# A decode attention block with its gradients: steps of two heads instead of four, with another order of work

## The chip, the cores and the metric

The kernel runs on one core of a Trainium2 chip. The core has five engines that run side by side, each through its own list of instructions in order: TensorE (PE, with a separate row PEld for its weight loads), VectorE (DVE), ScalarE (ACT), GpSimd (POOL) and SyncE (SP). SP and POOL here also issue the transfers, which 16 DMA engines carry out. The metric is the device time in microseconds (us), as a median of several executions. The profile shows one execution, and times in it count from its first instruction.

## The reference

One decode step (one token for each of two batches) of an attention block and a bilinear MLP beside it, and then the gradients with respect to all inputs. Both read the same normalized `x`.

```python
xn = layernorm(x)                                   # 2 x 576
q = (xn @ wq) as 32 heads of 128                    # two query heads per KV head
scores = q . k_cache / sqrt(128)                    # k_cache: 2 x 16 x 4096 x 128
p = softmax(scores);  o = p @ v_cache
out = x + o @ wo + ((xn @ w_gate) * (xn @ w_up)) @ w_down      # F = 4608
# and, from grad_out: gradients of x, k_cache, v_cache, wq, wo, w_gate, w_up, w_down
```

The caches are bf16, 32 MB each, and their gradients are as large. Each cache gradient is an outer product: for one KV head, 4096 x 128 numbers come from the two query rows with 4096 probabilities (for V) or score gradients (for K). So the kernel reads 92.48 MB and writes 92.48 MB. The arithmetic on a byte is small, but every number of the gradients has to pass through PSUM.

## The kernel before

**Steps.** `G = 4` KV heads of one batch make a step; there are `NGRP * Bq = 8` steps. Their order is a Python loop at the end of the kernel. A step does this:

1. `head_scores` (K): load a head as one 1 MB transfer (L469, issued by SP) into a tile of 128 partitions x 4096; transpose it in 32x32 blocks on VectorE (L102, tile `X`); add its scores into PSUM tile `ps_sc` with 16 matmuls (L475) whose weights `W` are 128x128 and whose moving side has 256 columns. All four heads go into one 128x256 tile.
2. `softmax`: maxima, exponential on ScalarE, sums; the probabilities `pr`, and their transpose `pT`, made by VectorE.
3. The same `head_scores` for V, which gives the gradient of the probabilities; `contract` (L488) multiplies V by `pT`, 32 matmuls a head, each writing one of four strips of 32 PSUM partitions. The strips are added up by an fp32 matmul with a constant, `contract_end` (L497, `R40`, four per call).
4. `dscores` makes the score gradients `ds` and `dsT`; then `contract` of K with `dsT`.
5. `outer_units`: the cache gradients. For one pair of blocks, four matmuls (L512) multiply 32 rows of `pr` or `ds` by 32 rows of `BD`, a masked copy of the queries or of the output gradient, with 512 columns. They fill two PSUM tiles `ps_o` of 128x1024, one for each `aa`, that is for each group of 32 rows; ScalarE (L93) or VectorE (L90) casts them into the store tiles `so`; `evac` chooses by a running sum of costs. When a tile is full, POOL issues the store of 1 MB (L519). It holds a quarter of the tokens of four heads, so that a piece of 2 KB is contiguous in memory.

```python
for h in range(2):
    for aa in range(2):
        a = 2 * A + aa
        nc.tensor.matmul(o[aa][:, h, :], lhsT=rows[32 * a:32 * a + 32, P * h:P * (h + 1)],
                         rhs=BD[t][32 * a:32 * a + 32, cq, :], start=True, stop=True)
```

**Around the steps.** `mlp_units` works through the MLP in nine slices of 512 columns, with loads (L272 to L275), transposes (`Xw`, `Xd`), matmuls and gradient stores `stw`, `std`, `stt`; `group_front` and `back_units` do the same for the slices of `wq` and `wo` (1152 KB and less, stores `stq`, `sto`). These units and the outer products lie in two lists, `side` and `outs`; `fill` takes some from each between the heads of a step.

**What sets the order.** The tile framework orders the instructions of each engine and inserts the waits. Buffers come from pools by tag: 11 tiles `nat` hold heads and weights alike, 2 tiles `X`, 4 tiles `st` for stores, and in PSUM 2 `m`, 2 `sc` and 2 `o`. `build_BD` makes `BD` by a matmul (L456), a ScalarE cast (L458) and four VectorE masks of 128x512 (L461). SP executes its loads in order: a load whose tile is not free holds those behind it.

Of the kernel before, what the change touches and what calls it, by code (L numbers as in the profile page):

```python
# [13 lines left out]
P = 128  # L14


def view(t, p0, np_, off, dims):

    (pstep, _), *_ = t.ap
    return bass.AP(t.tensor, t.offset + p0 * pstep + off, [[pstep, np_], *[list(d) for d in dims]])  # L20


@with_exitstack
def kernel(
# [30 lines left out]
    G = 4  # L55
    GH = 2 * G
    NGRP = Hkv // G
    NIT = NGRP * Bq
    NCH = Sk // P
    WW = 24 + P  # L60
# [7 lines left out]
    HD2 = D // 2  # L68

    const = ctx.enter_context(tc.tile_pool(name="const", bufs=1))  # L70
    sb = ctx.enter_context(tc.tile_pool(name="sb", bufs=1))
    ps = ctx.enter_context(tc.tile_pool(name="ps", bufs=1, space=bass.MemoryType.PSUM))

    def ps_m(shape, dtype=FP32):
        return ps.tile(list(shape), dtype, tag="m", bufs=2, name="ps_m")

    def ps_sc():
        return ps.tile([P, 256], FP32, tag="sc", bufs=2, name="ps_sc")

    def ps_o():  # L80
        return ps.tile([P, 2, 512], FP32, tag="o", bufs=2, name="ps_o")

    load = {"v": 0.0, "s": 0.0}

    def evac(out, in_, cols):
        cv = 0.16 + cols * 0.00104
        cs = 0.19 + cols * 0.00083
        if load["v"] + cv < load["s"] + cs:
            load["v"] += cv
            nc.vector.tensor_copy(out=out, in_=in_)  # L90
        else:
            load["s"] += cs
            nc.scalar.copy(out, in_)  # L93

    def dve(us):
        load["v"] += us

    def act(us):
        load["s"] += us
# [4 lines left out]
    def pairs(ap):  # L104
        return ap.bitcast(FP32)


    ident = const.tile([P, P], BF16, name="ident")
    make_identity(nc, ident[:])
    identf = const.tile([P, P], FP32, name="identf")  # L110
    nc.vector.tensor_copy(identf[:], ident[:])

    def sums(name, dims, off=0):

        n = dims[0][1]
        t = const.tile([P, n], FP32, name=name)
        nc.vector.reduce_sum(t[:], view(identf[:], 0, P, off, dims), axis=AX.X)
        return t

    R8 = sums("R8", [[1, 8], [8, 16]])  # L120
    G8 = const.tile([P, 16, 8], FP32, name="G8")
    nc.vector.tensor_copy(G8[:], view(R8[:], 0, P, 0, [[0, 16], [1, 8]]))
    R40 = sums("R40", [[1, 8], [40, 4]])
    F8 = sums("F8", [[1, 8], [32, 4]])
    Q4 = sums("Q4", [[32, 4], [1, 32]])
    C16 = sums("C16", [[8, 16], [1, 8]])
    maskc = const.tile([P, 4], FP32, name="maskc")
    nc.vector.reduce_sum(maskc[:], view(C16[:], 0, P, 0, [[1, 4], [4, 4]]), axis=AX.X)
    mask8 = const.tile([P, 4, 2], FP32, name="mask8")
    nc.vector.tensor_copy(mask8[:], view(Q4[:], 0, P, 0, [[1, 4], [0, 2]]))  # L130

    sel = const.tile([P, 4, 4, 32], BF16, name="sel")
    selA = const.tile([P, 4, 4, 32], BF16, name="selA")
    for be in range(4):
# [3 lines left out]
    nc.vector.memset(one1[:], 1.0)  # L138

    x_bf = sb.tile([2, D], BF16, tag="st", bufs=4, name="x_bf")  # L140
    nc.sync.dma_start(x_bf[:], A_x.rearrange("b s d -> (b s) d"))
    dy_bf = sb.tile([2, D], BF16, tag="st", bufs=4, name="dy_bf")
    nc.sync.dma_start(dy_bf[:], grad_out.rearrange("b s d -> (b s) d"))
    x_f = sb.tile([2, D], FP32, tag="X", bufs=2, name="x_f")
    nc.vector.tensor_copy(x_f[:], x_bf[:])

    mu = const.tile([2, 1], FP32, name="mu")
    nc.vector.reduce_sum(mu[:], x_f[:], axis=AX.X)
    nc.vector.tensor_scalar(mu[:], mu[:], 1.0 / D, None, op0=ALU.mult)
    xn_f = sb.tile([2, D], FP32, tag="nat", bufs=11, name="xn_f")  # L150
    nc.vector.tensor_scalar(xn_f[:], x_f[:], mu[:], None, op0=ALU.subtract)
    xsq = sb.tile([2, D], FP32, tag="X", bufs=2, name="xsq")
    var = const.tile([2, 1], FP32, name="var")
    nc.vector.tensor_tensor_reduce(
        out=xsq[:], in0=xn_f[:], in1=xn_f[:], scale=1.0 / D, scalar=0.0,
        op0=ALU.mult, op1=ALU.add, accum_out=var[:],
    )
    eps_t = const.tile([2, 1], FP32, name="eps_t")
    nc.vector.memset(eps_t[:], EPS)
    rstd = const.tile([2, 1], FP32, name="rstd")  # L160
    nc.scalar.activation(rstd[:], var[:], AF.Sqrt, bias=eps_t[:], scale=1.0)
    nc.vector.reciprocal(rstd[:], rstd[:])
    nc.vector.tensor_scalar(xn_f[:], xn_f[:], rstd[:], None, op0=ALU.mult)
    xn_bf = sb.tile([2, D], BF16, tag="st", bufs=4, name="xn_bf")
    nc.vector.tensor_copy(xn_bf[:], xn_f[:])

# [5 lines left out]
    for src, dst in ((dy_bf, dyr), (xn_bf, xnr)):  # L172
        o = ps_o()
        for k in range(2):
            nc.tensor.matmul(o[:, k, 0:HD2], lhsT=sel2[:].rearrange("b a m -> b (a m)"),
                             rhs=src[0:2, k * HD2:(k + 1) * HD2], start=True, stop=True)
        nc.vector.tensor_copy(dst[:].rearrange("p (k n) -> p k n", k=2), o[:, :, 0:HD2])


    xs = const.tile([P, 6, 32], BF16, name="xs")  # L180
    nc.gpsimd.memset(xs[:], 0.0)
    tp = ps_m([P, 6, 2], BF16)
    for c in range(4):
        nc.tensor.transpose(tp[:, c, :], xn_bf[0:2, c * P:(c + 1) * P], ident[0:2, 0:2])
    nc.tensor.transpose(tp[0:64, 4, :], xn_bf[0:2, 512:576], ident[0:2, 0:2])
    nc.tensor.transpose(tp[:, 5, :], xn_bf[0:2, 448:576], ident[0:2, 0:2])
    nc.vector.tensor_copy(xs[:, 0:4, 0:2], tp[:, 0:4, :])
    nc.vector.tensor_copy(xs[0:64, 4, 0:2], tp[0:64, 4, :])
    nc.vector.tensor_copy(xs[64:128, 5, 0:2], tp[64:128, 5, :])


    Wdy = const.tile([P, NB, 2, P], BF16, name="Wdy")
    nc.gpsimd.memset(Wdy[:], 0.0)
    dyT = sb.tile([P, 2 * NB, 32], BF16, tag="X", bufs=2, name="dyT")
    t32(dyT[:].rearrange("p k m -> p (k m)"), view(dyr[:], 0, P, 0, [[64, NB], [1, 2], [2, 32]]))
    for a in range(4):
        nc.vector.tensor_copy(
            view(Wdy[:], 32 * a, 32, 32 * a, [[P, 2 * NB], [1, 2]]), dyT[32 * a:32 * a + 32, :, 0:2])

    W = [const.tile([P, 4, G, WW], BF16, name=f"W{t}") for t in range(2)]  # L200
    dM = const.tile([P, 2, G, P], BF16, name="dM")
    for t in range(2):
        nc.gpsimd.memset(W[t][:], 0.0)
    nc.gpsimd.memset(dM[:], 0.0)
    BD = [const.tile([P, 4, G * Dh], BF16, name=f"BD{t}") for t in range(2)]
    Wms = [const.tile([P, 35, 8], BF16, name=f"Wm{i}") for i in range(2)]
    Wts = [const.tile([P, 19, 8], BF16, name=f"Wt{i}") for i in range(2)]
    oTs = [const.tile([P, 2, GH, 32], BF16, name=f"oT{i}") for i in range(2)]
    for t in (*Wms, *Wts, *oTs):
        nc.gpsimd.memset(t[:], 0.0)  # L210
    nwm = [0]


    acc = const.tile([P, 5, 2], FP32, name="acc")
    nc.vector.memset(acc[:], 0.0)
    accx = const.tile([P, 160], FP32, name="accx")
    nc.vector.memset(accx[:], 0.0)

    def nat(shape, name):
        return sb.tile(list(shape), BF16, tag="nat", bufs=11, name=name)  # L220

    def xtile(shape, name):
        return sb.tile(list(shape), BF16, tag="X", bufs=2, name=name)

    def stile(shape, name):
        return sb.tile(list(shape), BF16, tag="st", bufs=4, name=name)

    def tailtile(name):
        return sb.tile([P, FS], BF16, tag="stt", bufs=2, name=name)


    def stationaries(rep, half):

        i = nwm[0] % 2
        nwm[0] += 1
        Wm, Wt = Wms[i], Wts[i]
        nc.vector.tensor_tensor(
            view(Wm[:], 0, P, 0, [[8, 32], [2, 4], [1, 2]]), view(rep, 0, P, 0, [[2, 32], [0, 4], [1, 2]]),
            view(mask8[:], 0, P, 0, [[0, 32], [2, 4], [1, 2]]), ALU.mult)
        for h in range(2):  # L240
            off, dims = half(h)
            n = len(dims) > 1 and dims[0][1] or 1
            nc.gpsimd.tensor_copy(
                view(Wt[:], 64 * h, 64, 0, [[P // n, n], [1, P // n]]), view(Wm[:], 64 * h, 64, off, dims))
        dve(0.4)
        return Wm, Wt

    def dxn(Wm, Wt, X, pos, xoff, xstep):

        dp = ps_m([P, 160])  # L250
        for s in range(8):
            for q in range(4):
                nc.tensor.matmul(dp[32 * q:32 * q + 32, 0:P], lhsT=view(Wm[:], 0, P, 8 * pos(q, s), [[1, 32]]),  # L253
                                 rhs=view(X[:], 0, P, xoff(q, s), [[xstep, 4], [2, 32]]),
                                 start=(s == 0), stop=(s == 7))
# [6 lines left out]
        dve(0.35)  # L262


    def mlp_units(i):
        f0 = i * FS
        m = {}

# [67 lines left out]
        def outer_gu(w):  # L336
            def f():
                hb = m["hb"]
                if w == 0:
                    m["st"] = stile([P, 8, FS], "stw")  # L340
# [330 lines left out]
    def fill(no, ns):  # L671
        for _ in range(min(no, len(outs))):
            outs.pop(0)()
# [139 lines left out]
```

## Time and profile before

| what | value |
|---|---|
| median of 3 runs | 670.47 us (668.05 to 681.68) |
| span of the profiled execution | 666.9 us |
| mean granted TensorE clock in it | 0.716 |
| bytes read and written | 92.48 MB and 92.48 MB |
| mean transfer rate | 279 GB/s |
| scores (L475) | 1024 matmuls of 256 columns, 189.7 us busy |
| outer products of the caches (L512) | 512 matmuls of 512 columns, 173.3 us busy |
| ScalarE casts of 128x1024 for `so` | 222, 1019 ns each |
| VectorE transposes of K and V | 64, 2299 ns each |

A row of groups names the line, the engine, the operation, the tiles (output <- inputs) and the count; then the busy time, the mean of one instruction in ns, and the idle time ahead of them with what ended it. The rows in tenths cut the span into 40 equal slices; `PEclk` is the share of full speed that TensorE's clock was granted. The page's chain of waits is followed back from the last instruction. A matmul's end is modelled, and matmuls overlap, so its busy time is not its cost in a sequence; the distance from one start to the next is.

### The profile page before, as it was taken

The page shows a single profiled execution, that of the slowest core. Times are in us where ns is not written, and L with a number is a line of the kernel's source. Part 1 is how long each engine was busy: PE and PEld are TensorE (multiplying, and loading weights), DVE is VectorE, ACT ScalarE, POOL GpSimd, SP SyncE. Part 2 cuts the span into 40 slices and gives each one's busy share as a digit, 9 for nine tenths or more (in the row PEclk, how much of TensorE's full clock was granted, in tenths as well). Part 3 has the DMA queues.
Part 4 walks back from the last instruction along what each step waited for, and adds up shares of the span by engine and source line. Part 5 has one row for each costly group of instructions (what it writes and reads, how often), then busy time and mean ns, then how long its engine had stood idle before and what let it go on. Part 6 is the DMA issues. An engine that isn't in the chain of part 4 may idle for free.

```text
span 666.9 us, 14489 instructions
## 1 busy us (share of the span) xinstructions
PE 574.7 (86%) x6297; PEld 298.5 (45%) x6297; DVE 360.4 (54%) x499; ACT 330.7 (50%) x445; POOL 129.8 (19%) x252
## 2 busy tenths in 40 slices
PE   1679997897989999897999999899796999989954
PEld 1455553545534445444543454355553345453411
DVE  8686245546594246636484345637287134862245
ACT  0145655283555545374445635456362655645441
POOL 6131201131121121221122221112022111201111
PEclk9998868597886558598776557578597556885555
DMA  8965989559959879749949969829977688834355
GB/s 296 373 234 189 364 325 371 185 178 420 393 201 340 325 246 339 291 154 408 388 163 365 321 249 348 312 83 362 403 280 267 228 295 326 305 133 166 128 197 197
DMA packets 52824, 185.89 MB, mean 279 GB/s; under 512 B 4077, under 2 KB 19065, under 8 KB 44569
## 3 DMA queue, kind: packets, MB, share of 16 engines
q1 hardware_dynamic: 28392, 92.49, 38.4%
q0 software_dynamic: 24368, 92.48, 37.4%
q8 instruction: 49, 0.80, 0.5%
q14 instruction: 15, 0.11, 0.1%
HBM read 92.48 MB, written 92.48 MB: 277 GB/s over the span
## 4 chain that ended last, share of the span: by engine, by line
PE 49%; issue 15%; DMA 10%; ACT 9%; DVE 8%; POOL 1%; ACTq 0%; POOLq 0%; DVEq 0%
PE ps_o L512 16%; PE ps_sc L475 14%; DMA out_dram<-so 10%; ACT so L93 7%; PE ps_m L488 5%; DVE X L102 3%; PE ps_m L497 2%; PE ps_o L379 2%; PE ps_o L345 2%; DVE so L90 1%; PE ps_m L253 1%; PE ps_m L417 1%; DVE Xw L102 1%; PE ps_o L655 1%; DVE stq L90 1%
## 5 line engine op out<-in xcount | busy, mean ns | idle before, releaser
L93 ACT CAST so<-ps_o 128x1024 bf16<-128x1024 f32 x222 | 217.1, 1019 | 174.2 <-PE ps_o L512 116.7
L475 PE MATMUL ps_sc<-X,W 128*128 128x256 bf16 x1024 | 189.7, 328 | 13.2 <-DVE negb L540 7.7
L102 DVE STREAM_TRANSPOSE X<-kv 128x2048 f32<-128x2048 f32 x64 | 147.0, 2299 | 47.0 <-PE ps_sc L475 21.1
L475 PEld LDWEIGHTS <-W 128*128 128x128 bf16 x1024 | 103.9, 113 | 82.8 <-issue 55.2
L512 PE MATMUL ps_o<-BD,pr 32*128 32x512 bf16 x256 | 91.6, 488 | 6.2 <-ACT so L93 4.4
L512 PE MATMUL ps_o<-BD,ds 32*128 32x512 bf16 x256 | 81.7, 487 | 12.0 <-ACT so L93 3.5
L519 POOL DMA_DIRECT2D out_dram<-so x64 | 48.9, 765 | 193.9 <-ACT so L93 91.8
L90 DVE CAST so<-ps_o 128x1024 bf16<-128x1024 f32 x34 | 41.4, 1218 | 49.1 <-PE ps_o L512 43.3
L488 PE MATMUL ps_m<-kv,dsT 128*32 128x128 bf16 x1024 | 29.4, 285 | 11.4 <-ACT o_sb L491 11.4
L93 ACT CAST stw<-ps_o 128x1024 bf16<-128x1024 f32 x33 | 32.6, 1017 | 11.6 <-PE ps_o L345 9.7
L488 PE MATMUL ps_m<-kv,pT 128*32 128x128 bf16 x1024 | 38.2, 257 | 0.1
L488 PEld LDWEIGHTS <-pT 128*32 128x32 bf16 x1024 | 20.3, 107 | 36.1 <-issue 33.5
L488 PEld LDWEIGHTS <-dsT 128*32 128x32 bf16 x1024 | 23.1, 128 | 29.3 <-issue 27.7
L512 PEld LDWEIGHTS <-ds 32*128 32x128 bf16 x256 | 14.7, 96 | 37.3 <-issue 32.0
L497 PEld LDWEIGHTS ps_m<-R,o_sb 128*128 128x128 f32 x128 | 25.7, 281 | 11.0 <-issue 5.7
L93 ACT CAST std<-ps_o 128x576 bf16<-128x576 f32 x33 | 20.7, 640 | 18.8 <-PE ps_o L379 14.4
L497 PE MATMUL ps_m<-R,o_sb 128*128 128x2 f32 x128 | 27.7, 321 | 2.6 <-DVE cr L566 2.6
L512 PEld LDWEIGHTS <-pr 32*128 32x128 bf16 x256 | 15.7, 97 | 25.3 <-issue 16.9
L491 ACT COPY o_sb<-ps_m 128x128 f32<-128x128 f32 x64 | 17.0, 278 | 20.1 <-PE ps_m L488 19.8
L458 ACT CAST bd<-ps_m 128x512 bf16<-128x512 f32 x16 | 9.4, 587 | 30.7 <-PE ps_m L456 30.6
L379 PE MATMUL ps_o<-dyr,hb 32*128 32x288 bf16 x72 | 19.3, 365 | 4.8 <-ACT std L93 4.7
L261 DVE TENSOR_TENSOR accx<-accx,ps_m 128x160 f32<-128x160 f32 x13 | 4.0, 309 | 35.9 <-PE ps_m L258 35.9
(180 smaller groups left out, 578.4 us busy)
## 6 DMA issues: line engine op xcount, KB each, us to landing
out_dram<-so POOLq DMA_DIRECT2D x64, 1024.0 KB, 7.5
kv<-in_A_k_cache_dram SPq DMA_DIRECT2D x32, 1024.0 KB, 8.4
kv<-in_A_v_cache_dram SPq DMA_DIRECT2D x32, 1024.0 KB, 8.8
out_dram<-stw POOLq DMA_DIRECT2D x18, 512.0 KB, 8.1
wd<-in_B_w_down_dram SPq DMA_DIRECT2D x9, 576.0 KB, 8.2
out_dram<-std POOLq DMA_DIRECT2D x9, 576.0 KB, 4.4
wo<-in_A_wo_dram SPq DMA_DIRECT2D x4, 1152.0 KB, 9.4
wgu<-in_B_w_gate_dram SPq DMA_DIRECT2D x9, 512.0 KB, 9.9
```

Of the source, the lines that this page charges most:

```text
L90: nc.vector.tensor_copy(out=out, in_=in_)
L93: nc.scalar.copy(out, in_)
L102: nc.vector.transpose(out, in_)
L345: nc.tensor.matmul(o[a // 2][:, a % 2, dc * P:(dc + 1) * P], lhsT=xnr[32 * a:32 * a + 32, dc * P:(dc + 1) * P], rhs=hb[32 * a:32 * a + 32, ...
L379: nc.tensor.matmul(o[aa][:, k, 0:HD2], lhsT=hb[32 * a:32 * a + 32, 0, :], rhs=dyr[32 * a:32 * a + 32, k * HD2:(k + 1) * HD2], start=True, ...
L458: nc.scalar.copy(bd[:], bp[:].rearrange("p l d -> p (l d)"))
L475: nc.tensor.matmul(s_ps[:], lhsT=view(W[t][:], 0, P, (be * G + l) * WW + 24 - 8 * cq, [[1, P]]), rhs=view(X[:], 0, P, 2 * cq * Dh + 64 * ( ...
L488: nc.tensor.matmul(o_ps[32 * cq:32 * cq + 32, :], lhsT=rowsT[:, 4 * h + c4, :], rhs=head[:, 8 * c4 + 2 * cq + h, :], start=(h == 0 and c4 ...
L491: nc.scalar.copy(o_sb[:, l, :], o_ps[:])
L497: nc.tensor.matmul(t_ps[:, 2 * l:2 * l + 2], lhsT=o_sb[:, l, :], rhs=R40[:, 2 * l:2 * l + 2], start=True, stop=True)
L512: nc.tensor.matmul(o[aa][:, h, :], lhsT=rows[32 * a:32 * a + 32, P * h:P * (h + 1)], rhs=BD[t][32 * a:32 * a + 32, cq, :], start=True, sto ...
L519: nc.gpsimd.dma_start(oview[b, 2 * A + aa, :, G * g:G * g + G], m["st"][aa][:].rearrange("p l c d -> p l (c d)"))
```

## The change

Most of the kernel is written anew. What it does:

- `G = 2`: a step has two heads of K and two of V, and there are 16 steps.
- **Scores in four column tiles.** `score` issues 32 matmuls a head with weights of 32 columns and a moving side of 128; four in a row (`cq`) write the four strips of 32 partitions of one 128x128 PSUM tile.
- **`spread`** replaces the VectorE transposes of `pr` and `ds`: 32 small matmuls with a permuted identity make both the transposed and the spread rows; one cast takes them from PSUM (`pp`, `dd`).
- **Contraction** of both V heads and both K heads in one go at the end of the step, each in one column tile, with two columns of weights; one fp32 matmul a step follows. The four head tiles are released after it.
- **Head stores.** A store tile holds one head as it lies in memory: one partition has 32 tokens, 8 KB. The unit of the outer product has two matmuls for two groups of 32 rows, into the two halves of one PSUM tile. The store is issued by SP.
- **`BD`** is made in one GpSimd product of 128x2048 for a step and side.
- **Fixed rings** in place of pools: 9 head tiles `kv`, 5 weight tiles `ww`, 1 `gu`, 3 `X`, 4 `st`, 3 `BD`, in PSUM 2 `o`, 2 `m`, 1 `sk`, 1 `sv`.
- **Order.** Every part is a Python generator that yields what it needs (an engine with a cost, a free slot, an event). The class `Order` advances them by a list schedule with these costs, while the kernel is built; under `manual_schedule` the instructions of an engine keep that order on the chip.

```diff
+class Order:
+    HOP = 0.12
+    BW = 410e3
+    SLACK = 0.15
...
+    def run(self):
+        while self.streams:
...
+            t0 = min(c[0] for c in cand)
+            t, s, e = min((c for c in cand if c[0] <= t0 + self.SLACK), key=lambda c: (c[1].prio, c[0]))
...
+def EV(cols, bias=0.25):
+    return ("any", [("ACT", 0.19 + cols * 0.00083, 0.0), ("DVE", 0.16 + cols * 0.00104, bias)])
...
+NKV, NX, NGU, NWW, NST, NBD = 9, 3, 1, 5, 4, 3
+MLP0, MLPD = 5, 6.5
+KVSTORE = "SP"
...
-    G = 4
+    G = 2
...
+    def put(engine, parts, tag, slot, events=()):
+        def run():
+            for j, (dst, src, nbytes) in enumerate(parts):
+                yield DMA(engine, 0.77 if engine == "POOL" else 0.6, nbytes)
+                (nc.gpsimd if engine == "POOL" else nc.sync).dma_start(dst, src)
+            yield ("lrel", tag, slot)
...
+    def unit(mms, pe, cols, ev, store):
+        i = yield ACQ("o")
+        yield PE(pe)
+        mms(o_t[i])
+        e = yield EV(cols)
+        ev(e, o_t[i])
+        yield REL("o", i)
+        yield from store.done()
...
+    def load_kv():
...
+                    i = yield ACQ("kv")
+                    yield DMA("SP", 0.6, 1 << 20)
+                    nc.sync.dma_start(kv_t[i][:], views[t][b, G * g + l])
...
+                    for h in range(2):
+                        yield DVE(1.25)
+                        t32(pairs(X_t[x][:, 2048 * h:2048 * h + 2048]), pairs(src[:, 2048 * h:2048 * h + 2048]))
...
+                yield POOL(4.5)
+                nc.gpsimd.tensor_tensor(BD_t[i][:], view(vr_t[v][:], 0, P, 0, [[0, 16], [1, Dh]]),
+                                        view(mask16[:], 0, P, 0, [[1, 16], [0, Dh]]), ALU.mult)
...
+    def score(t, s, sc, l):
...
+        for be in range(4):
+            for c2 in range(2):
+                for cq in range(4):
+                    nc.tensor.matmul(
+                        sc[32 * cq:32 * cq + 32, :],
+                        lhsT=view(W[:], 0, P, (be * G + l) * WW + 6 - 4 * c2 - 2 * l, [[1, 32]]),
+                        rhs=view(X[:], 0, P, (2 * cq + c2) * Dh + 64 * (be // 2) + be % 2, [[8 * Dh, 4], [2, 32]]),
...
+    def spread(src, dst_ps):
+        for c4 in range(4):
+            for a in range(4):
+                blk = src[:, 32 * c4:32 * c4 + 32]
+                rows = identP[:, 32 * a:32 * a + 32]
+                nc.tensor.matmul(dst_ps[32 * a:32 * a + 32, 32 * c4:32 * c4 + 32], lhsT=blk, rhs=rows,
+                                 start=True, stop=True)
...
+    def head_outer(s, t, l, pr2, done):
+        i = yield ACQ("st")
...
+        store = Store(4, put(KVSTORE, [(oviews[t][b, G * g + l], st[:], 1 << 20)], "st", i, ()))
+        def mk(A, h2):
+            def mms(o):
+                for k in range(2):
+                    c4 = 2 * A + k
+                    nc.tensor.matmul(o[:, k, :], lhsT=pr2[32 * c4:32 * c4 + 32, :],
+                                     rhs=BD[32 * c4:32 * c4 + 32, 8 * l + 4 * h2:8 * l + 4 * h2 + 4, :],
+                                     start=True, stop=True)
...
+    def contract(s):
...
+        heads = [(S["ppT"], kvS[s][1][l], l) for l in range(G)] + [(S["ddT"], kvS[s][0][l], l) for l in range(G)]
+        for part in range(4):
+            yield PE(0.95)
...
+            for c in range(8 * part, 8 * part + 8):
+                for j, (rT, slot, l) in enumerate(heads):
+                    nc.tensor.matmul(ct[32 * j:32 * j + 2, 0:P], lhsT=rT[:, 4 * c + 2 * l:4 * c + 2 * l + 2],
+                                     rhs=kv_t[slot][:, Dh * c:Dh * (c + 1)], start=False,
+                                     stop=(c == NCH - 1), skip_group_check=True)
+        for t in range(2):
+            for l in range(G):
+                yield REL("kv", kvS[s][t][l])
...
+    with tc.manual_schedule():
+        od.spawn(front(), (-1.0,))
+        od.spawn(load_ws(), (-0.5,), 1.2)
+        od.spawn(load_kv(), (0.0,), 1.2)
+        od.spawn(turn(), (1.0,))
...
+        od.spawn(attend(), (0.0,))
+        od.spawn(dscores(), (0.0,))
+        od.spawn(backs(), (1.2,))
+        od.run()
```

The arithmetic stays the same, as do the bytes read and written.

## Prediction

> **What bounds the kernel now.** I read the busy row, then the clock and DMA rows, then the queues and the chain that ended last.
>
> ```profile
> PE 574.7 (86%) x6297; PEld 298.5 (45%) x6297; DVE 360.4 (54%) x499; ACT 330.7 (50%) x445; POOL 129.8 (19%) x252
> ...
> PEclk9998868597886558598776557578597556885555
> DMA  8965989559959879749949969829977688834355
> ...
> q1 hardware_dynamic: 28392, 92.49, 38.4%
> q0 software_dynamic: 24368, 92.48, 37.4%
> ...
> PE 49%; issue 15%; DMA 10%; ACT 9%; DVE 8%; POOL 1%; ACTq 0%; POOLq 0%; DVEq 0%
> ```
>
> TensorE is busy for 86%, often at a granted clock of half speed. The transfers need 38.4% + 37.4% + 0.6% = 76.4% of the span, 509 us of 666.9. So the DMA engines are the floor, and 158 us of their time is lost. Windows of 10 us (columns: us, PE, PEld, DVE, ACT, POOL busy, clock, DMA share, GB/s) show where:
>
> ```profile
> 130.00:140.00 10.00, 9.79 (x100) 5.49 (x99) 2.99 (x4) 5.44 (x6) 1.42 (x6) 0.76 0.01 2
> ...
> 150.00:160.00 10.00, 8.32 (x136) 5.43 (x135) 8.50 (x13) 4.50 (x6) 2.15 (x5) 0.83 1.02 424
> ...
> 220.00:230.00 10.00, 10.00 (x110) 4.84 (x106) 2.87 (x7) 6.67 (x9) 2.23 (x3) 0.50 1.00 352
> 230.00:240.00 10.00, 10.00 (x71) 3.69 (x71) 4.58 (x6) 4.16 (x6) 1.90 (x6) 0.50 0.52 200
> ```
>
> While TensorE is full, DMA goes from saturated to nothing. The reader is to see that the two hinder each other. SyncE's own waits name the link:
>
> ```profile
> SPq L469 <- PE ps_m L488: 171.4, 29, 20.2
> SPq L469 <- DVE Xw L102: 72.9, 4, 24.2
> ```
>
> A head's load waits 171 us in all for the contraction that frees its buffer. A step holds 8 heads, and the 11 `nat` buffers are shared with the weights.
>
> **TensorE, part by part.** The spacing of matmuls comes from pieces of the chain (start, length, what), all in stretches at clock 0.5:
>
> ```profile
> 133.20 0.97 PE ps_o L512 x4
> ...
> 226.47 0.96 PE ps_o L512 x2
> ...
> 392.64 2.57 PE ps_m L488 x92
> ...
> 402.76 3.31 PE ps_sc L475 x15
> ```
>
> *Scores.* 1024 matmuls of 256 columns, 3.31/15 = 0.22 us each: 225 us if all ran at half clock. They become 2048 of 128 columns in four column tiles. L488 has that shape, 2.57/92 = 0.028 us, so 57 us; minus 168. The trace mixes clocks (189.7 us busy), so in it they shrink to about 48.
>
> *Outer products.* Still 512 matmuls of 512 columns. Two of them cost 0.96 us now when both use the same 32 rows (`h` runs inside one PSUM tile), but four cost 0.97 when row groups alternate. The new unit always pairs two row groups into one PSUM tile: 256 pairs at 0.485, 124 us at half clock; against 173.3 in the mixed trace, about 95.
>
> *Smaller.* The fp32 reduction L497 falls from 128 matmuls (27.7 us) to 16: 5 us. The 1024 new matmuls of 32 columns in `spread` have a near row, L258 (32 columns, column tiles): 16 in 0.26 us; 16 us, at most 29 if they cost like L488. Sixteen short softmax chains instead of eight add 32 fp32 matmuls, 0.3 us each: 10. The rest keeps its work, 574.7 - 189.7 - 173.3 - 27.7 = 184 us. Sum 48 + 95 + 5 + 16 + 10 + 184 = **358 us**; at half clock throughout (184 becomes about 220), 57 + 124 + 8 + 25 + 10 + 220 = **444**. Both lie under the DMA floor, so TensorE stops being the bound, whichever clock is granted.
>
> **The other engines.** ScalarE: the order of its instructions in the changed kernel has 284 evacuations of 1024 columns (264 now) at 1.019, 289 us, 61 of 576 at 0.64, 39, and some 40 us of small copies and exponentials: about 370 against 330.7. VectorE loses the 64 masks (19.1) and the transposes of probabilities (7); halving the K and V transposes costs 64 fixed shares, (2 x 1373 x 1024/1152 - 2299) ns = 0.14 us each, 9 us; double chains add 18, and 13 fewer large casts take 16 away: about 345. GpSimd gets 32 products of 128x2048 that no row shows. Below, its memset of 128x2432 takes 2.27 us, so 1.9. The Trainium skill, "GPSIMD Engine Reference", section on elementwise cost, prices a two-input product of 2048 fp32 elements at 4.5 us; I take that, and twice it as the upper end: 144 us, 61 to 288. With 49 us of head stores gone from its queue, POOL stands near 230. Three BD buffers put these products beside the previous step.
>
> **A rule against this.** The skill's "SBUF — State Buffer", section "two separate sides", says that a GpSimd operation locks a port pair, and VectorE operations with two SBUF inputs or in a two-port mode wait for all of it. The row first: the K transpose runs at 2299/2048 = 1.12 ns per element, the pace of casts out of PSUM (1218/1024 = 1.19), so it shows no use of a second port. The exposed operations are 33 small ones (`pr`, `hb`, `qr`). By the rule GpSimd holds the lock for 144/560 of the time, mean rest 2.25 us: 33 x 0.26 x 2.25 = 19 us of VectorE; by the rows, nothing. VectorE has 200 us spare; both leave the total.
>
> **DMA.** The bytes are unchanged, 185 MB. Loads in mostly 8 KB rows cost 38.4% for 92.49 MB, stores in 2 KB pieces 37.4% for 92.48: long rows buy nothing measurable; I take zero, with 3% of the stores' share (8 us) for the ends. The skill's "DMA: Bandwidth & Descriptors", specifications, limits a core to about 358 GB/s from HBM; that would make 185/0.358 = 517 us. The windows with DMA share about 1 run at 352 to 426, most near 375 to 400; 375 gives 493. I take the row.
>
> What matters is whether loads can run on. A step now holds 4 heads, and 9 buffers are theirs alone: while one step waits for its contraction, five heads of the next ones can land. Waiting for L488 should mostly go. Next late is the queue itself.
>
> **Moved work.** The 64 head stores leave POOL for SP. SP executes in order: a store waiting for ScalarE holds every load and weight behind it, and a load waiting for PE holds the stores. The order gives four loads, then about four stores, so each delay is one burst. In the same ring a store also lands after the loads ahead of it. The four `st` buffers are filled 107 times (64 heads, 43 weight gradients): over 535 us each filling may last 20. It fills in 4 x 1.02 us, is issued in 0.8, and lands in 7.5 now (page, head stores), say 13 behind part of a burst: 18. It fits, barely.
>
> **The sum.** After the last exponential ScalarE's order still holds 57 casts of 1024 columns and 13 of 576, 58 + 8 + 3 for small ones = 69 us. The last store and the final row arithmetic follow: from the last `stqt` cast at 655.8 to the end it is 11 us now; with a 1 MB landing, 16. Tail 85 us, against 73 now (no score matmul after 594). In those 69 us some 20 MB move. Before them 166 MB must move: 166/0.375 = 443 us, plus 4 us of a slow start. For in-order waits I add 5% of it, 25 us. 4 + 443 + 25 + 85 = **557 us of span**. The executed median is 670.5 for a span of 666.9, so 3.6 lie around it: **560 us**, 110 us less. If the stalls vanish it is 535; if head stores are truly cheaper, 527; with 15% stalls, 602.
>
> **Rivals.**
> *One ring, four store buffers* (slower). If a store regularly lands behind a whole burst of 4 heads and 1.6 MB of weights, that is 5.6/0.375 = 15 us more: hold 4.1 + 0.8 + 22.5 = 27.4, and 107 x 27.4/4 = 733 us. It decides over the DMA from a hold of about 21, and passes today's time at 25. For it: ScalarE waits already 13.2 us for `out_dram<-so`, and that link is 10% of the chain. Against it: the stores overlap three other fillings, and bursts are half as long as steps today.
> *Part of the idle stays* (less gain). Loads still come in fours after a contraction that frees K and V together; if bulk transfer runs at 320 GB/s, between today's mean of 279 and full: 166/0.32 + 89 + 4 = 612.
> *It doesn't do what it says.* The waits only move to SP behind stores and DMA stays at today's 280 to 290: 166/0.285 + 93 = 675, near no change. Against it: the buffer count per step more than doubles.
>
> **Chances.** Forecast (527 to 602) 0.62; 612 case 0.20; no change 0.07; one-ring case 0.11. Range 520 to 640, which leaves out the last two. Two per cent, 657 to 684, is what a measurement of this kernel can tell from no change: faster 0.82, same 0.07, slower 0.11.
>
> **What would show it.** Right: score matmuls near 30 ns apart, PE busy below 450 us, DMA share above 85% before the tail, few SP waits on the contraction, ScalarE closing the kernel for about 70 us. Wrong: ScalarE or VectorE waiting for `out_dram<-st` by more than 60 us (one ring), GpSimd products above 9 us, DMA windows below 0.1 in mid-kernel, or head stores landing in more than 20 us.

## The result, and the profile after

Time after: **639.16 us** median of 4 runs (633.71 to 640.21), against 669.26 us for the kernel before in the same session. The ratio is 0.957, with a 95% interval of 0.949 to 0.965. Some executions of the kernel before are in a slower state, and the ratios here and below compare the others. The kernel is faster by 4%, where 16% were forecast: 30 us of 110. The profiled execution has a span of 638.4 us, at a mean granted TensorE clock of 0.584 (0.716 before).

The rows of the page after, the same ones that the prediction shows of before:

```profile
PE 452.2 (71%) x8489; PEld 270.5 (42%) x8489; DVE 355.1 (56%) x643; ACT 344.5 (54%) x470; POOL 204.8 (32%) x289
...
PEclk9976565765557565755555565655557555556555
DMA  8949989693998749986963969896938965493661
...
q1 hardware_dynamic: 40424, 159.61, 65.4%
q0 software_dynamic: 7024, 25.37, 10.4%
```

TensorE lost 122 us of busy time, although its clock fell. The transfers need about the same share as before: 65.4% + 10.4%, and 0.8% for two small queues, are 76.6%, 489 us instead of 509. No row of an engine is full, and yet only 29 us of span are gone. The waits of SyncE's queue after:

```profile
SPq L477 <- ACT st L309: 226.1, 37, 19.3
...
SPq L810 <- PE ps_o L953: 31.9, 4, 18.0
...
SPq L810 <- PE ps_o L508: 21.0, 3, 9.2
SPq L810 <- PE ps_m L939: 16.2, 2, 8.3
SPq L810 <- PE ps_m L1092: 10.7, 2, 6.1
SPq L810 <- PE ps_m L1000: 9.2, 2, 8.9
```

Only one of these rows names the contraction (L1092), but the names mislead. The profile infers who ended a wait from what TensorE was doing just then. A head tile `kv` is read by TensorE in the contraction alone, and the times agree. Here is one case, the last matmuls of a contraction and the next head load (start us, us, what):

```profile
233.53 0.22 PE L1092 MATMUL ps_m<-kv,dd 128*2 128x128 bf16 x2
...
233.80 0.34 SPq L810 DMA_DIRECT2D kv<-in_A_k_cache_dram  x1
```

All 13 waits of over 1 us ahead of a head load, 97 us together, end within 0.05 us of the end of a contraction, that of two steps before. In the kernel before, 209 us of such waits end so. They are halved, then, and not gone, and the heads still come in bursts of about four. Ahead of them in the queue stand the stores (L477), which wait for their casts. Whether that costs anything, the first experiment tells.

**Where the time is.** I cut each span at the end of the last exponential, as the prediction did: 588 us before, 535 us after. The windows (us, busy time of PE, PEld, DVE, ACT, POOL, clock, DMA share, GB/s) of before:

```profile
0.00:588.00 588.00, 517.96 (x5751) 275.12 (x5751) 327.03 (x447) 297.94 (x403) 118.04 (x234) 0.74 0.81 296
588.00:667.00 79.00, 56.76 (x549) 23.43 (x547) 33.35 (x53) 32.74 (x42) 11.81 (x18) 0.55 0.42 153
```

and of after:

```profile
0.00:535.00 535.00, 382.04 (x7583) 239.00 (x7583) 318.81 (x576) 280.20 (x393) 179.51 (x266) 0.60 0.81 307
535.00:638.00 103.00, 70.17 (x908) 31.48 (x906) 36.30 (x68) 64.25 (x79) 25.29 (x23) 0.52 0.55 215
```

The first part became 53 us shorter, and the tail gave 24 us of it back. In the tail ScalarE has 64 us of work instead of 33: the outer products that the list ranks last have piled up there (100 of the 512 matmuls of L953, where 64 of L512 were left before). In the first part TensorE went from 88% busy to 71%, so its freed time became idle time, not speed. The transfers still run at a mean share of 0.81.

One piece of TensorE's timeline after (start us, us, what, idle time before it and its releaser) shows what it does in such idle time:

```profile
384.70 0.61 PE L953 MATMUL ps_o<-BD,pp 32*128 32x512 bf16 x2 [0.42 <-ACT st L309]
385.61 0.61 PE L953 MATMUL ps_o<-BD,pp 32*128 32x512 bf16 x2 [0.30 <-ACT st L309]
386.52 0.61 PE L953 MATMUL ps_o<-BD,pp 32*128 32x512 bf16 x2 [0.31 <-ACT st L309]
387.44 0.61 PE L953 MATMUL ps_o<-BD,pp 32*128 32x512 bf16 x2 [0.31 <-ACT st L309]
```

A unit of two matmuls comes every 0.91 us, not every 0.485. There are two PSUM tiles `o`, and each is free again only when its cast has ended. TensorE works in order, so all that is listed behind the unit stands with it. The window row of this stretch, and VectorE's next instruction, tell what sets the pace:

```profile
384.50:388.30 3.80, 2.44 (x8) 0.44 (x9) 0.00 (x0) 3.80 (x5) 1.08 (x2) 0.50 0.94 335
...
392.00 1.23 DVE L311 CAST st<-ps_o 128x1024 bf16<-128x1024 f32 x1 [9.08 <-DMA out_dram<-st]
```

ScalarE casts for all of the 3.80 us, one cast every 0.90 us, and VectorE does nothing: its next cast waits 9.08 us for a store to land and free its store tile. So in this burst the casts on one engine are the limit, and more PSUM tiles alone would not have made it quicker. From 376 to 438 us no score is computed at all; bursts like this one, MLP and projection work, and waits for their weights fill that stretch.

### The profile page after: what moved, and what is told of

Read it like the earlier page. It is cut to its first block, busy times and chain, and to the rows that moved or that the text cites. A ratio compares the mean times of both kernels' runs of the same rounds, so it can differ in the third digit from the quotient of the medians.

```text
span 638.4 us, 19297 instructions
## 1 busy us (share of the span) xinstructions
PE 452.2 (71%) x8489; PEld 270.5 (42%) x8489; DVE 355.1 (56%) x643; ACT 344.5 (54%) x470; POOL 204.8 (32%) x289
## 3 DMA queue, kind: packets, MB, share of 16 engines
q1 hardware_dynamic: 40424, 159.61, 65.4%
q0 software_dynamic: 7024, 25.37, 10.4%
## 5 line engine op out<-in xcount | busy, mean ns | idle before, releaser
L309 ACT CAST st<-ps_o 128x1024 bf16<-128x1024 f32 (+1 forms) x345 | 310.6, 958 | 155.9 <-PE ps_o L953 74.8
L909 POOL TENSOR_TENSOR BD<-vr,mask 128x2048 bf16<-128x2048 bf16 x32 | 115.1, 3598 | 150.0 <-PE ps_o L953 102.5
L305 DVE STREAM_TRANSPOSE X<-kv 128x1024 f32<-128x1024 f32 x128 | 152.1, 1218 | 10.3 <-DMA kv<-in_A_k_cache_dram 6.0
L953 PE MATMUL ps_o<-BD,dd 32*128 32x512 bf16 x256 | 71.8, 592 | 31.1 <-ACT st L309 29.9
L953 PE MATMUL ps_o<-BD,pp 32*128 32x512 bf16 x256 | 68.5, 551 | 26.2 <-ACT st L309 25.5
L477 POOL DMA_DIRECT2D out_dram<-st x43 | 33.2, 771 | 94.1 <-ACT st L309 87.7
L921 PEld LDWEIGHTS <-W 128*32 128x32 bf16 x2048 | 50.4, 132 | 25.7 <-issue 22.7
L1092 PE MATMUL ps_m<-kv,dd 128*2 128x128 bf16 x1024 | 53.7, 286 | 5.0 <-issue 5.0
L1092 PE MATMUL ps_m<-kv,pp 128*2 128x128 bf16 x1024 | 53.6, 286 | 3.0 <-issue 3.0
L1092 PEld LDWEIGHTS <-pp 128*2 128x2 bf16 x1024 | 45.0, 111 | 8.5 <-issue 7.0
L1092 PEld LDWEIGHTS <-dd 128*2 128x2 bf16 x1024 | 45.0, 111 | 5.9 <-issue 5.9
L953 PEld LDWEIGHTS <-dd 32*128 32x128 bf16 x256 | 15.0, 103 | 63.3 <-issue 57.5
L953 PEld LDWEIGHTS <-pp 32*128 32x128 bf16 x256 | 14.7, 99 | 58.8 <-issue 55.3
L477 POOL DMA_DIRECT2D out_dram<-tl x26 | 14.6, 563 | 33.0 <-ACT tl L309 33.0
```

Source lines behind the costliest of these rows:

```text
L305: nc.vector.transpose(out, in_)
L477: (nc.gpsimd if engine == "POOL" else nc.sync).dma_start(dst, src)
L909: nc.gpsimd.tensor_tensor(BD_t[i][:], view(vr_t[v][:], 0, P, 0, [[0, 16], [1, Dh]]), view(mask16[:], 0, P, 0, [[1, 16], [0, Dh]]), ALU.mult)
L921: nc.tensor.matmul(sc[32 * cq:32 * cq + 32, :], lhsT=view(W[:], 0, P, (be * G + l) * WW + 6 - 4 * c2 - 2 * l, [[1, 32]]), rhs=view(X[:], 0 ...
L953: nc.tensor.matmul(o[:, k, :], lhsT=pr2[32 * c4:32 * c4 + 32, :], rhs=BD[32 * c4:32 * c4 + 32, 8 * l + 4 * h2:8 * l + 4 * h2 + 4, :], star ...
L1092: nc.tensor.matmul(ct[32 * j:32 * j + 2, 0:P], lhsT=rT[:, 4 * c + 2 * l:4 * c + 2 * l + 2], rhs=kv_t[slot][:, Dh * c:Dh * (c + 1)], start= ...
```

## The experiments

All are edits of the changed kernel. Each was timed in 4 runs beside 7 runs of the kernel before on one chip (675.21 us median of all seven); the ratios are to that kernel, as is the 0.957 of the changed one. The changed kernel was timed at another time, so the ratios are what to compare. The last column cuts the profiled span at the last exponential.

| kernel | median us | ratio, 95% interval | span = first part + tail, us |
|---|---|---|---|
| changed kernel | 639.16 | 0.957 (0.949 to 0.965) | 638.4 = 535.0 + 103.4 |
| stores on ScalarE's queue | 653.41 | 0.975 (0.966 to 0.984) | 653.9 = 553.1 + 100.8 |
| 1/8 of the cache traffic | 589.26 | 0.878 (0.870 to 0.887) | 584.2 = 484.6 + 99.6 |
| half outer matmuls | 634.12 | 0.947 (0.937 to 0.956) | 630.0 = 528.8 + 101.2 |
| 1/8 of the GpSimd product | 628.94 | 0.939 (0.929 to 0.949) | 624.8 = 524.9 + 99.9 |

### Does SyncE's in-order queue hold the loads back?

```diff
-                (nc.gpsimd if engine == "POOL" else nc.sync).dma_start(dst, src)
+                (nc.gpsimd if engine == "POOL" else nc.scalar).dma_start(dst, src)
```

> The head stores and the weight-gradient stores are issued by ScalarE's queue instead of SyncE's, in the same places of the same list; the loads then have SyncE's queue to themselves. Queue theory (SyncE's in-order waits for casts, 226 us of them before stores, hold the loads behind them and make the gaps in the transfers): the loads run up to 20 us earlier, the time falls to about 580 us (between 560 and 605). TensorE theory (the steps are as long as TensorE at half clock and the casts between its outer products make them): within 2% of 639 us. A cost on the other side: ScalarE issues 64 large stores and waits for VectorE's casts in order, which could add about 64 x 0.5 us = 30 us to its own chain.

The edit moved the 64 head stores alone; the weight-gradient stores stayed on POOL's queue. Measured: 653.41 us, slower; the interval of its ratio begins where that of the changed kernel ends. SyncE's longest waits in it:

```profile
SPq L843 <- DVE X L305: 122.0, 6, 58.4
SPq L810 <- PE ps_o L508: 83.9, 3, 30.4
SPq L810 <- PE ps_o L953: 75.5, 4, 29.3
```

With the stores gone from the queue, the loads (L810, L843) wait as long, now for their own buffers. The names of the rows mislead here too. The head loads (L810) wait 293 us in 13 waits that each end within 0.05 us of the end of a contraction. Here is the one of the same step as above:

```profile
237.14 0.22 PE L1092 MATMUL ps_m<-kv,dd 128*2 128x128 bf16 x2
...
237.41 0.33 SPq L810 DMA_DIRECT2D kv<-in_A_k_cache_dram  x1
```

The load had stood at the head of the queue for 34 us, and is issued 3.6 us later than in the changed kernel. None of the 13 comes more than 0.4 us earlier than there. So the 226 us of store waits held back no head load that could have run: **the queue theory is refuted**. What holds the heads is the contraction at the end of a step, and nine tiles for heads are not enough to run past it. The slowdown has the size of the side cost that was named. ScalarE issues in order, and its next cast follows late:

```profile
205.49 0.34 ACTq L477 DMA_DIRECT2D out_dram<-st  x1
205.92 1.01 ACT L309 CAST st<-ps_o 128x1024 bf16<-128x1024 f32 x1 [0.47 <-ACT st L309]
```

64 x 0.47 = 30 us on ScalarE, and the first part is 18 us longer (553.1 - 535.0). That it is this cost is argued from its size alone. The Trainium skill, "Trainium Kernel Development and Optimization", section "Key Constraints", says that spreading transfers over several queues saves only issue time, since all share the 16 DMA engines. This run gained nothing from the second queue, but for another reason, the loads' own buffers, so it does not test that sentence. What it shows is that the issue time moved to an engine that has casts to do.

### Do the transfers set the pace?

```diff
-                    nc.sync.dma_start(kv_t[i][:], views[t][b, G * g + l])
+                    w = NCH * Dh if n < NKV else 512
+                    nc.sync.dma_start(kv_t[i][:, 0:w], views[t][b, G * g + l][:, 0:w])
...
-        store = Store(4, put(KVSTORE, [(oviews[t][b, G * g + l], st[:], 1 << 20)], "st", i, ()))
+        store = Store(4, put(KVSTORE, [(oviews[t][b, G * g + l][:, 0:512], st[:, 0:512], 1 << 20)], "st", i, ()))
```

> Leaves out 7/8 of each cache load after the first nine and 7/8 of each head store (112 MB of 134 MB of cache traffic); all instructions and their order stay. Transfer theory (the 443 us of the forecast's sum: transfers at 375 GB/s set the pace of the steps): the time falls by 100 us or more, to 500 us or less. TensorE theory: what is left is TensorE's own chain with its casts, and the time stays at 600 us or above. Between these, 500 to 600 us, both take part, and the fall is what the transfers add on top.

Measured: 589.26 us, between the two. It moves 77 MB instead of 186. One thing more than the traffic changes: a head load that overwrites 512 columns need not wait for the whole contraction, and is issued 2 to 5 us before its end (at 79.42 us for instance, end at 81.62). The windows of this kernel:

```profile
0.00:485.00 485.00, 373.77 (x7584) 235.38 (x7584) 314.75 (x577) 279.58 (x393) 180.04 (x266) 0.62 0.42 140
485.00:584.00 99.00, 68.71 (x906) 30.92 (x906) 35.96 (x67) 63.76 (x78) 25.33 (x23) 0.55 0.27 94
```

With DMA at 0.42 the first part still takes 485 us, more than the 472 that the prediction gave the full transfers. So **a second floor lies as high as that of the transfers**, and taking the traffic away buys 50 us there and 4 in the tail. TensorE is busy for 77% of that part; the rest are waits inside the list, the largest of them for ScalarE's casts (31.4 us below). Where the 50 us enter is suggested by the waits that end with a transfer; they lie on several engines and do not add up to a time. The changed kernel, first part (engine, line, what it waits for: us, times, longest):

```profile
DVE X L305 <- DMA ww<-in_B_w_down_dram: 24.6, 4, 9.2
ACT st L309 <- DMA out_dram<-st: 20.6, 7, 7.5
DVE st L311 <- DMA out_dram<-st: 18.6, 3, 9.1
PE ps_m L570 <- DMA gu<-in_B_w_gate_dram: 9.1, 3, 4.7
PE ps_m L570 <- DMA gu<-in_B_w_up_dram: 7.2, 4, 2.6
...
DVE X L305 <- DMA kv<-in_A_k_cache_dram: 6.0, 3, 3.6
...
DVE X L305 <- DMA kv<-in_A_v_cache_dram: 1.2, 2, 0.9
```

and the first part with 1/8 of the cache traffic:

```profile
PE ps_o L954 <- ACT st L309: 31.4, 73, 1.1
...
DVE X L305 <- DMA ww<-in_B_w_down_dram: 8.6, 4, 5.2
...
PE ps_m L570 <- DMA gu<-in_B_w_up_dram: 2.8, 3, 1.4
PE ps_m L570 <- DMA gu<-in_B_w_gate_dram: 2.0, 1, 2.0
```

The heads of the cache are late by only 7 us in the changed kernel (26 us before, for the same transposes). What is late are MLP weights, and free store tiles, 39 us. Both shrink or vanish with the traffic. The longest of the weight waits shows that the place in the queue counts as well:

```profile
421.30 0.58 SPq L850 DMA_DIRECT2D ww<-in_B_w_down_dram  x1
...
430.26 1.38 DVE L305 STREAM_TRANSPOSE X<-ww 128x1152 f32<-128x1152 f32 x1 [9.19 <-DMA ww<-in_B_w_down_dram]
```

The load stands behind the loads into the one tile `gu` and is issued only when its reader is already free (VectorE has been idle since 421.07). A second `gu` tile, or this load ahead of the others, was not tried.

### Do TensorE's outer products set it?

```diff
-                    nc.tensor.matmul(o[:, k, :], lhsT=pr2[32 * c4:32 * c4 + 32, :],
-                                     rhs=BD[32 * c4:32 * c4 + 32, 8 * l + 4 * h2:8 * l + 4 * h2 + 4, :],
+                    nh = 4 if s < 2 else 2
+                    nc.tensor.matmul(o[:, k, 0:nh * Dh], lhsT=pr2[32 * c4:32 * c4 + 32, :],
+                                     rhs=BD[32 * c4:32 * c4 + 32, 8 * l + 4 * h2:8 * l + 4 * h2 + nh, :],
```

> Leaves out half of the columns of each outer product's matmuls after the first two steps (256 instead of 512); casts, stores, loads and order stay. The group of four takes 0.97 us at half clock in the profile of after, 140 us busy in all, so about 66 us of TensorE's time go. TensorE theory: the time falls by 40 to 70 us, to 570 to 600 us. Transfer theory and queue theory: under 2% change, for the casts and the queue are as they were.

Measured: 634.12 us. The ratio's interval overlaps that of the changed kernel, so no effect is shown, and the 570 to 600 us of the TensorE theory are missed. TensorE's own busy time did fall, by 40.5 us (452.2 to 411.7; 66 were expected). In the groups of the changed kernel (busy us, mean ns | idle time before and its releasers)

```profile
L953 PE MATMUL ps_o<-BD,dd 32*128 32x512 bf16 x256 | 71.8, 592 | 31.1 <-ACT st L309 29.9 <-DVE st L311 0.3
L953 PE MATMUL ps_o<-BD,pp 32*128 32x512 bf16 x256 | 68.5, 551 | 26.2 <-ACT st L309 25.5
```

and of this one

```profile
L954 PE MATMUL ps_o<-BD,dd 32*128 32x256 bf16 (+1 forms) x256 | 48.8, 407 | 40.4 <-ACT st L309 38.6 <-DVE st L311 1.4
L954 PE MATMUL ps_o<-BD,pp 32*128 32x256 bf16 (+1 forms) x256 | 48.6, 382 | 33.7 <-ACT st L309 31.8 <-DVE st L311 1.0 <-ACT tl L309 0.3
```

the busy time falls by 42.9 us, and the idle time before the same matmuls grows by 16.8, nearly all of it for ScalarE's casts. So the length of these matmuls isn't the bound, and a good part of what they lose turns into waiting for PSUM. That agrees with units paced by their casts, as in the burst above. The counter-test, halving the casts or halving both, was not run, and neither was another rank for these units in the list. What makes the floor of 485 us, the casts or the list's order of short dependent steps, therefore **stays open**.

### Does the GpSimd product cost anything?

```diff
-                nc.gpsimd.tensor_tensor(BD_t[i][:], view(vr_t[v][:], 0, P, 0, [[0, 16], [1, Dh]]),
-                                        view(mask16[:], 0, P, 0, [[1, 16], [0, Dh]]), ALU.mult)
+                nb = 16 if s < 2 else 2
+                nc.gpsimd.tensor_tensor(BD_t[i][:, 0:nb, :], view(vr_t[v][:], 0, P, 0, [[0, nb], [1, Dh]]),
+                                        view(mask16[:], 0, P, 0, [[1, nb], [0, Dh]]), ALU.mult)
```

> Leaves out 7/8 of GpSimd's product after the first two steps (2 of 16 blocks; 3.6 us becomes about 0.5 us); everything else stays. GpSimd theory (the product lengthens the path from the probabilities to the outer products, and shares VectorE's port): the time falls by 15 to 40 us. All other theories: under 2% change (626 to 652 us), since the product is built ahead in one of three buffers.

Measured: 628.94 us. The span is 13.6 us shorter, just short of the 15 expected, and the median lies inside the 626 to 652 us of the other theories. The ratio's interval (0.929 to 0.949) ends where that of the changed kernel begins, so the effect is small and only just clear of noise. What it does to VectorE is plain. VectorE, none of whose instructions was changed, is busy for 335.9 us instead of 355.1. The instructions around `ex`, durations in ns as least/median/most, in the changed kernel

```profile
L1020 DVE TENSOR_SCALAR pr<-ex,rz x16: 246/288/3515, 34.8 to 536.9; 128x128 bf16<-128x128 f32 x16
```

and with the small product

```profile
L1021 DVE TENSOR_SCALAR pr<-ex,rz x16: 244/286/293, 35.0 to 526.7; 128x128 bf16<-128x128 f32 x16
```

show how: most `pr` are as quick as ever, but 6 of the 16 take from 0.7 to 3.5 us, up to the length of one GpSimd product (3.6 us). That fits the lock of the shared port in the prediction's rule. TensorE waits for the late `pr` (10.2 us, only 0.5 with the small product). Whether the rest of the 13.6 us comes from the lock or from an earlier `BD`, this run can't separate.

## Why the prediction was right or wrong

The sign held, and so did the range, but by less than 1 us of its upper end (640), which is luck; the size did not, nor did the mechanism at the loads. The sum had 472 us up to the last exponential and 85 after it; measured are 535.0 and 103.4. The miss of 81 us is 63 + 18.

- **TensorE's work: right.** The sum for half clock was 444 us, and the page shows 452.2 at a clock of 0.584. Scores: 32 matmuls from 520.01 to 520.99 us of the timeline are 31 ns each; 28 were forecast. Outer products, four in a row: 1.03 us in most places (from 517.72 us on, for instance), 0.97 forecast. The other engines' sums held within 11%: ScalarE 344.5 us (370 forecast), VectorE 355.1 (345), GpSimd 204.8 (230).
- **"Both lie under the DMA floor, so TensorE stops being the bound": the step that failed.** It compared sums of separate engines and took the largest. With most of the cache traffic gone the first part still lasts 485 us, while TensorE's work in it is 374. Between the two stand waits of TensorE on other engines' results, which no sum of busy times holds. The outer product was priced at the spacing of its matmuls (0.485 us), but in a burst it costs the cast that must follow it (0.91). TensorE's waits for casts ahead of L953 are 55.4 us; ahead of L512 before, casts of ScalarE and VectorE ended some 16. What in these waits makes the floor of 485 us stays open.
- **Transfers, 443 us and 29 of waits and start: the transfers right, the waits mis-sized.** A DMA share of 0.81 over 535 us is 433 us of transfers; the other 102 us are the term that had 29. "Waiting for L488 should mostly go" failed: 97 us of head loads' waits still end with a contraction (209 before), and with the stores gone from the queue 293 did. That "five heads of the next ones can land" is true, but then the tiles are full. It costs little by itself, for head tiles are late by only 7 us. "Next late is the queue itself" does not hold for the stores either: taking them out made the kernel slower. Late instead are weights and store tiles. The 50 us that traffic still costs lie on a floor of 485, so the first part is neither 472 nor 485 but 535.
- **Store ring, "fits barely": nearly right.** Stores land in 6.1 us (13 forecast), and ScalarE and VectorE wait 39.2 us for store tiles, under the 60 that would have made it the bound. The slower rival doesn't decide, yet part of its mechanism is in the 50 us.
- **Tail: 85 forecast, 103.4 measured.** The last row arithmetic is right: the last cast ends at 623.3, and 15 us follow (16 forecast). ScalarE's 69 us were right as work, 64.25 us busy. But they were taken as back to back: ScalarE is idle for the other 24 of the 88 us, mostly for TensorE, which has a score, two contractions and MLP work between the units. This term was mis-sized by 18 us.
- **Port lock: the rule pointed the right way, "both leave the total" did not hold.** The rule gave 19 us on VectorE, and 19.2 went with the product. That they agree so closely is luck: with the measured 3.6 us in place of 4.5 the same sum, over the 535 us, gives about 13. The row of transposes and casts gave nothing, and these are indeed unchanged (1218 ns). Spare time on VectorE did not hide it, because `pr` lies in the chain that TensorE waits for. The product itself took 3.6 us, not 4.5.
- **The rival "part of the idle stays" (612 us)** came nearest in time, and it had the transfers right: loads do come in fours after a contraction, and the first part runs at 307 GB/s, where it took 320. But the heads that come so are late by only 7 us. What the bursts cost was not tested; more head tiles, or an earlier release of them, would show it.
- **Signs named in advance.** 3.6 us products and score spacing came as in the right case. TensorE's 452 us just missed the 450, and the waits on the contraction were halved rather than few. The two that failed clearly, a DMA share of 0.81 instead of 0.85 before the tail and a ScalarE that closes the kernel with gaps, stand for the two terms of the miss.

## What to carry to other kernels

When a change takes a bottleneck engine below its neighbours, do not read the new time as the largest of the engines' sums: first price each unit by the slowest engine that it must pass before its buffer is free (here the cast, 0.91 us and not 0.485), in the order in which the engines must wait. Then ask of each transfer which consumer is late for it; a long wait on a queue, like the 226 us of stores here, can hold back nothing. Check the name that a profile gives to a wait against the times at which the possible causes end. And look at what a scheduler ranks last, because it returns as a tail: 24 of the 53 us won were given back there.

## What the runs showed of the hardware

- TensorE's granted clock was lower with less work. Over the first part it was 0.74 at 88% busy before and 0.60 at 71% after. From 460 to 480 us of the changed kernel TensorE is busy for 17.4 of 20 us at a clock of 0.52. Most of its matmuls there use 32 rows, 32 columns or 2 columns of the array. That the kind of matmul is the cause is a guess; no run varied it alone.
- A two-input GpSimd product can cost a VectorE instruction up to the product's whole length: `pr` took 288 ns in the median and 3515 at most beside products of 3.6 us, and 293 at most beside those of 0.6 us.
- GpSimd's bf16 product of 128x2048 took 3600 ns, and that of 128x256 took 610. A straight line through the two gives a fixed part of about 0.18 us and 1.67 ns per element, as an estimate.
- A 1 MB store issued by ScalarE occupies 0.34 us of its queue, and its next cast starts 0.47 us after the last one ended (both also the medians of the 64 stores).
